# Moving operands as even and odd columns in two halves, read in turn by TensorE

## The chip, the cores and the metric

The kernel runs on one core of one Trainium2 chip. The metric is the device time of one execution in microseconds, as the median of several runs. Of one execution there is a hardware profile: a page, and a trace with every instruction's start and duration.

## The reference

A gated mix of an attention block and a gated feed-forward block over the same 2048 tokens of 512 numbers. 32 query heads of 16 share one key head and one value head; the feed-forward block is 1792 wide. Everything is float32.

```python
g = sigmoid((x * gate_w).sum(-1, keepdims=True))
q = (x @ wq).reshape(B, S, 32, 16).transpose(0, 2, 1, 3)
k, v = x @ wk, x @ wv
p = softmax(einsum("bhqd,bkd->bhqk", q, k) * 16 ** -0.5)
a = einsum("bhqk,bkd->bhqd", p, v).transpose(0, 2, 1, 3).reshape(B, S, 512) @ wo
b = (sigmoid(x @ w_gate) * (x @ w_up)) @ w_down
return g * a + (1 - g) * b
```

## The kernel before

**Numbers in two parts.** A float32 operand is split into a rounded part (type float32r, "hi") and the rest ("lo"), and a product is made as three products of these parts: hi x hi, hi x lo, lo x hi. The tiles that hold both parts have the shape [128, 2, 512]. float32r products are read by TensorE at one column after another without a second pass; plain float32 products show in the trace as two instructions each.

**Full-array products.** `project` (line 864) makes keys, values, the gate and the queries of a block of 512 tokens: 12 products of 128 rows by 512 moving columns, with `X[b, kc]` as the moving operand. `query_out` has ScalarE copy the queries out of PSUM; `store_q` sends them to memory, and `load_q` brings them back, stacked three times, into `stage`, which `stack` splits into `qs`.

**Paired products.** All else but the values uses one half of the array's rows (64 partitions), and two products, one on each half, go side by side as a pair:

- `maximum` (line 1126): 128 queries as the stationary operand against 512 keys (`ks`, moving); VectorE reduces each result of 128 x 512 to its row maxima (line 1128).
- `scores` (line 1135): 128 keys (stationary) against 512 queries (`qs`, moving), with the maxima subtracted by way of extra rows; ScalarE takes the exponential (line 1137) and writes `p`.
- `fill` (line 1105): gate and up products (`w` stationary, `x` or its copy with the halves exchanged, `xs`, moving), down products (`h` stationary, `wd` moving) and the attention's output products (`o` stationary, `wo` moving). ScalarE and VectorE take the results from PSUM (`gate`, `gated`, `part_of`).

**Values.** `pv` (line 1010) multiplies `p` (plain float32, 128 rows, moving) by `v_aug` in four column groups of the array, 32 columns each, side by side; eight instructions for one chunk of 128 keys and four heads. They come in runs of one to five chunks. Transposes (lines 934, 995) lie between them.

**Order.** A planner was run beforehand, and its outcome is a string `ORDER`, one character a step: `G` a full-array group, `V` a chunk of values, `C` the end of a sum, `T` the turning of maxima, and a hexadecimal digit for a pair, which tells what each half does (1 `maximum`, 2 `scores`, 3 `fill`). `plan()` goes through the string with costs for each engine and writes out the order of all instructions; at the end, each engine's instructions are chained in that order. The string, and thus the order, doesn't depend on what the chip does in a run: a step whose bank isn't free waits. PSUM has eight banks, each the target of one product group at a time, and a bank comes free when VectorE or ScalarE has read it.

**Layout.** `kernel` prepares the inputs on the host: x transposed in blocks of 512 tokens, the gate and up weights cut into column blocks, wo and wd as they are. Rows of 512 lie contiguously in SBUF, and the moving read goes through them from the first to the last.

Of the kernel before, what the change touches and what calls it, by code (L numbers as in the profile page):

```python
# [17 lines left out]
S, D, H, DH, F = 2048, 512, 32, 16, 1792  # L18
P = 128
TB = 512  # L20
NB = S // TB
NT = TB // P
KC = D // P
# [703 lines left out]
def tile_kernel(ctx, tc, x_in, wq, wkv, wo, wg, wu, wd, consts_in, out):  # L727
    nc = tc.nc
# [13 lines left out]
    banks = [pp.tile([P, 512], F32, tag=f"bank{i}", name=f"bank{i}") for i in range(8)]  # L742
# [18 lines left out]
    X, XS, XR = {}, {}, {}  # L761
# [48 lines left out]
    RAWS, WS = {}, {}  # L810
# [35 lines left out]
                hl = wp.tile([P, 2, 512], F32R, tag="wd", name=f"{name}_{k}", bufs=DB)  # L846
                WS[kind, b, 2 * i + k] = split(raw[r, k, :], hl[r], nc.gpsimd.tensor_copy, nc.gpsimd)

    full = slice(0, 512)
    part = lambda i: slice(i * P, (i + 1) * P)  # L850

    THREE = ((0, 0), (0, 1), (1, 0))
# [6 lines left out]
    def project(ps, w, b, order=BY_W, between=()):  # L859

        for i, (kc, (p, q)) in enumerate(order):
            if i < len(between):
                early(between[i])
            nc.tensor.matmul(ps, w[:, p, part(kc)], X[b, kc][:, q, :], start=i == 0, stop=i == 3 * KC - 1)  # L864


    wkv_c = fp.tile([P, TB], F32, tag="gs", name="wkv_raw", bufs=2)[:, :KC * 33]
# [15 lines left out]
    def early(n):  # L883

        for _ in range(n):
            nc.tensor.matmul(banks[7][:, :P], v_aug[:, :4, :], v_aug[:, 4:8, :], start=True, stop=True)
# [14 lines left out]
    ks = cp.tile([P, S], F32R, name="ks")  # L901
# [3 lines left out]
    qs_t = [cp.tile([P, 2, TB], F32R, name=f"qs{i}") for i in range(3)]  # L905
# [12 lines left out]
    def keys(b, _, ps):  # L918
        if b == 0:
            project(ps, wkv_s, b, BY_X, EARLY)  # L920
        else:
            project(ps, wkv_s, b)
# [26 lines left out]
    QD = {}  # L949

    def query(b, t, ps):
        project(ps, wq_s[t], b)

    def query_out(b, t, ps):
        QD[b, t] = ap.tile([P, TB], F32, tag="p", name=f"q{b}_{t}", bufs=PB)
        nc.scalar.copy(QD[b, t], ps)  # L956

    def store_q(b, t):

# [134 lines left out]
    def fill(h, j, at, i):  # L1094
        c, (p, q) = at // 3, THREE[at % 3]
        half = HALF[h]
        if j.kind in "gu":


            l, r = WS[j.key][half, p, part(c)], (X if c % 2 == h else XS)[j.b, c // 2][half, q, :]  # L1100
        else:
            c += 2 * FG[j.i // NT][0] if j.kind == "d" else KC - 1 if j.kind == "e" else 0
            l = (HS if j.kind == "d" else OT)[j.b, c][half, p, part(j.i % NT)]
            r = WS[j.kind, j.b, 0 if j.kind == "e" else c][half, q, :]
        nc.tensor.matmul(banks[i], l, r, start=at == 0, stop=at == j.n - 1)  # L1105

    def gate(h, j, i):
        GS[j.b, j.i, h] = fp.tile([P, TB], F32, tag="gs", name=f"gs{j.b}_{j.i}_{h}", bufs=2)
# [12 lines left out]
    def maximum(h, n, i):  # L1121
        s, pr = divmod(n, 2)
        u, n = divmod(s, NC)
        qt, kb = divmod(n, 4) if u else (n % 4, n // 4)
        r = slice(64 * h, 64 * h + 62)
        nc.tensor.matmul(banks[i], qs_t[u % 3][r, pr, part(qt)], ks[r, kb * 512:(kb + 1) * 512],  # L1126
                         start=True, stop=True)
        nc.vector.tensor_reduce(MX[u][:, pr, h, qt, kb:kb + 1], banks[i], axis=AX.X, op=ALU.max)  # L1128

    def scores(h, n, i):  # L1130
        e, pr = divmod(n, 2)
        pr = 1 - pr
        u, c = divmod(e, NC)
        r = HALF[h]
        nc.tensor.matmul(banks[i], ks[r, part(c)], qs_t[u % 3][r, pr, :], start=True, stop=True)  # L1135
        p = PT[u, c, 2 * pr + h] = ap.tile([P, 512], F32, tag="p", name=f"p{u}_{c}_{pr}_{h}", bufs=PB)
        nc.scalar.activation(p, banks[i], AF.Exp, scale=0.25)  # L1137

    on_bank = lambda act: lambda *args: act(*args[:-1], banks[args[-1]])
    acts = {  # L1140
        "load_x": first_x, "x_first": first_hi, "xf": first_lo, "wq_first": wq_hi, "wq": wq_lo, "keys": on_bank(keys),
        "query": on_bank(query), "turn": on_bank(turn), "keys_out": on_bank(keys_out), "query_out": on_bank(query_out),
        "turned": on_bank(turned), "store_q": store_q, "load_q": load_q, "stack": stack,
        "load": load_item, "w_hi": w_hi, "w": w_split, "x_hi": x_hi, "x": x_lo, "turn_x": turn_x,
        "f": fill, "gate": gate, "gated": gated, "h": h_split, "part": part_of, "add": add_part, "out": send_out,
        "m": maximum, "max_finish": max_finish, "max_turn": max_turn, "send_max": send_max, "s": scores,
        "values": on_bank(pv), "sums_out": on_bank(sums_out), "sum_add": sum_add, "store": store, "sums": sums, "invert": invert, "send_inverse": send_inverse,
        "spread": spread, "divide": divide,
# [10 lines left out]
    ps = rest[3:]  # L1159
# [5 lines left out]
    o = []  # L1165
# [9 lines left out]
        nc.scalar.copy(o[i], rest[2 - i][:, 2 * P:3 * P])  # L1175
    for t in range(NT):
        r = HALF[t % 2]
        nc.tensor.matmul(ps[t], o[t // 2][r], WS["last"][r], start=True, stop=True)  # L1178
    for t in (0, 1, 2, 3):

        ba, scale = BA[NB - 1, t], gsig[:, n0 + t:n0 + t + 1]
# [10 lines left out]
    last = {}  # L1192
# [46 lines left out]
```

## Time and profile before

| | |
|---|---|
| median of 3 runs | 1591.24 us (1591.23 to 1591.73) |
| span of the profiled execution, first to last instruction | 1588.7 us |
| TensorE busy, weight loads busy | 1580.4 us, 1003.2 us |
| VectorE, ScalarE, GpSimd busy | 1410.7, 1186.8, 905.5 us |
| mean granted clock of TensorE | 1.000 |
| moved by DMA | 98.13 MB |

The profile's page gives the span, which leaves out what lies before the first and behind the last instruction; the runs' times hold it. A busy TensorE means that a product was under way, not that the array took a column at every clock: products are pipelined, and the start of one to the start of the next says more than a duration. In the rows, PE is TensorE's products, PEld its weight loads, DVE VectorE, ACT ScalarE, POOL GpSimd. A group's row gives the line, the engine, the operation, the tiles as out<-in, the shapes, the count, then busy time in us and the mean duration in ns, and the engine's idle time ahead of these instructions with what ended it. A timeline row gives start and duration in us. A row of stretches gives, for each engine, the busy time and the count of instructions, then the granted clock, the share of the DMA engines' time and GB/s.

### The profile page before, as it was taken

How to read it: one execution, taken by the hardware profiler on the slowest of the kernel's cores; microseconds unless marked ns; L12 is line 12 of the kernel's file. 1: busy time of each engine (PE TensorE's matmuls, PEld its weight loads, DVE VectorE, ACT ScalarE, POOL GpSimd, SP SyncE). 2: the span in 40 equal slices, each digit the busy share in tenths (PEclk: the TensorE clock that was granted, in tenths of full speed). 3: DMA queues.
4: the chain of work that ended last, by engine and by line, in shares of the span. 5: the costliest groups of instructions: out<-in, count | busy, mean ns of one | idle time of the engine just before them, and what ended most of it. 6: DMA issues, size and time to landing. Idle time of an engine off the chain costs nothing.

```text
span 1588.7 us, 33698 instructions
## 1 busy us (share of the span) xinstructions
PE 1580.4 (99%) x12950; PEld 1003.2 (63%) x12950; DVE 1410.7 (89%) x2450; ACT 1186.8 (75%) x2349; POOL 905.5 (57%) x703
## 2 busy tenths in 40 slices
PE   9999999999999999999999999999999999999998
PEld 7767666556655666665755666666565566666644
DVE  6999899999899999998988989998998998989962
ACT  5277767688688767788769776788877876777897
POOL 5347565756753664675582666465766366468242
PEclk9999999999999999999999999999999999999999
DMA  7312111123110221114121211111512021110011
GB/s 239 138 49 75 55 37 41 59 68 101 52 58 23 86 63 40 55 42 109 51 72 32 84 43 55 35 58 32 134 32 81 24 83 59 29 59 31 9 35 45
DMA packets 52231, 98.13 MB, mean 62 GB/s; under 512 B 17960, under 2 KB 19240, under 8 KB 51044
## 3 DMA queue, kind: packets, MB, share of 16 engines
q1 hardware_dynamic: 52068, 95.96, 19.7%
q8 instruction: 102, 1.67, 0.4%
q14 instruction: 61, 0.50, 0.1%
HBM read 74.05 MB, written 8.90 MB: 52 GB/s over the span
## 4 chain that ended last, share of the span: by engine, by line
PE 99%; DMA 0%; ACT 0%; SPq 0%; DVE 0%; issue 0%; DVEq 0%; ACTq 0%
PE bank L1105 33%; PE bank L1010 30%; PE bank L1126 16%; PE bank L1135 16%; PE bank L864 3%; DMA wqr<-wq 0%; PE bank L995 0%; PE bank L1178 0%; SPq L767 0%; PE bank L934 0%; ACT x L782 0%; DVE ba L1187 0%; DVEq L1235 0%; ACT wq L910 0%; ACT q L956 0%
## 5 line engine op out<-in xcount | busy, mean ns | idle before, releaser
L1128 DVE TENSOR_REDUCE mx<-bank 128x1 f32<-128x512 f32 x2048 | 1261.2, 683 | 114.5 <-PE bank L1126 62.2
L1137 ACT ACTIVATE p<-bank 128x512 f32<-128x512 f32 x2048 | 1032.5, 656 | 35.6 <-PE bank L1135 18.6
L1135 PE MATMUL bank<-qs,ks 64*128 64x512 f32 x2048 | 713.7, 405 | 0.0
L1126 PE MATMUL bank<-ks,qs 62*128 62x512 f32 x2048 | 691.1, 405 | 0.0
L1010 PE MATMUL bank<-p,v_aug 128*32 128x512 f32 x4096 | 485.1, 598 | 0.0
L1135 PEld LDWEIGHTS bank<-qs,ks 64*128 64x128 f32 x2048 | 350.5, 185 | 133.2 <-DVE mx L1128 44.1
L1126 PEld LDWEIGHTS bank<-ks,qs 62*128 62x128 f32 x2048 | 348.6, 185 | 112.0 <-DVE mx L1128 31.3
L1018 ACT COPY ou<-bank 128x512 f32<-128x512 f32 x131 | 77.1, 589 | 299.1 <-PE bank L1010 236.2
L1105 PE MATMUL bank<-wd,hl 64*128 64x512 f32 x1344 | 272.2, 391 | 0.0
L1010 PEld LDWEIGHTS bank<-p,v_aug 128*32 128x32 f32 x4096 | 110.6, 109 | 248.5 <-issue 214.1
L1105 PEld LDWEIGHTS bank<-wd,hl 64*128 64x128 f32 x1344 | 199.0, 185 | 15.3 <-DVE mx L1128 0.2
L1021 POOL TENSOR_TENSOR ou<-ou,ou 128x512 f32<-128x512 f32 x104 | 134.3, 1292 | 98.3 <-ACT ou L1018 94.5
L1105 PE MATMUL bank<-xs,wg 64*128 64x512 f32 x672 | 184.6, 391 | 0.0
L1105 PE MATMUL bank<-xs,wu 64*128 64x512 f32 x672 | 183.7, 392 | 0.0
L1105 PE MATMUL bank<-x,wg 64*128 64x512 f32 x672 | 182.4, 391 | 0.0
L1105 PE MATMUL bank<-x,wu 64*128 64x512 f32 x672 | 181.3, 393 | 0.0
L982 POOL TENSOR_TENSOR qs<-stage,qs 16x1024 fp32r<-16x1024 f32 x62 | 148.4, 2393 | 4.8
L1105 PEld LDWEIGHTS bank<-x,wu 64*128 64x128 f32 x672 | 111.0, 185 | 10.2 <-DVE mx L1128 1.7
L1105 PEld LDWEIGHTS bank<-x,wg 64*128 64x128 f32 x672 | 112.5, 185 | 6.7
L1105 PEld LDWEIGHTS bank<-xs,wu 64*128 64x128 f32 x672 | 112.6, 185 | 6.4
L1105 PEld LDWEIGHTS bank<-xs,wg 64*128 64x128 f32 x672 | 112.3, 185 | 5.6
L757 POOL CAST hl<-h 128x512 fp32r<-128x512 f32 x56 | 34.2, 611 | 142.4 <-DVE h L1115 142.2
(92 smaller groups left out, 1159.6 us busy)
## 6 DMA issues: line engine op xcount, KB each, us to landing
rg<-wg SPq DMA_DIRECT2D x28, 512.0 KB
ru<-wu SPq DMA_DIRECT2D x28, 512.0 KB
rd<-wd SPq DMA_DIRECT2D x28, 512.0 KB
stage<-qd SPq DMA_DIRECT2D x192, 64.0 KB
xs<-x SPq DMA_DIRECT2D x16, 512.0 KB
xf<-x_in SPq DMA_DIRECT2D x16, 256.0 KB
qd<-q SPq DMA_DIRECT2D x16, 256.0 KB
ra<-wo SPq DMA_DIRECT2D x8, 512.0 KB
```

The source lines that it names most:

```text
L757: hi(hl[:, 0, :], raw)
L864: nc.tensor.matmul(ps, w[:, p, part(kc)], X[b, kc][:, q, :], start=i == 0, stop=i == 3 * KC - 1)
L982: e.tensor_tensor(qs[r], stage[r], f32(qs[r]), op=ALU.subtract)
L1010: nc.tensor.matmul(ps[32 * j:32 * j + 32, :], v_aug[:, c, :], PT.pop((u, c, j)), start=new, stop=last)
L1018: (nc.scalar.copy if e == "act" else nc.vector.tensor_copy)(OU[i], ps)
L1021: nc.gpsimd.tensor_tensor(OU[n], OU[n], OU[i], op=ALU.add)
L1105: nc.tensor.matmul(banks[i], l, r, start=at == 0, stop=at == j.n - 1)
L1126: nc.tensor.matmul(banks[i], qs_t[u % 3][r, pr, part(qt)], ks[r, kb * 512:(kb + 1) * 512], start=True, stop=True)
L1128: nc.vector.tensor_reduce(MX[u][:, pr, h, qt, kb:kb + 1], banks[i], axis=AX.X, op=ALU.max)
L1135: nc.tensor.matmul(banks[i], ks[r, part(c)], qs_t[u % 3][r, pr, :], start=True, stop=True)
L1137: nc.scalar.activation(p, banks[i], AF.Exp, scale=0.25)
```

## The change

The moving operands of `project`, `fill`, `maximum`, `scores` and the last output products are read through `turned_round`, a view of a row of 512 as 256 x 2 with the step of 256 innermost: TensorE reads element 0, 256, 1, 257, and so on. For x, wo and wd the host lays out the rows so that even columns fill the first half and odd ones the second, and the products come out in natural order as before. The queries are put into that layout by the ScalarE copy in `query_out`, whose destination is now written in turn in two halves (PSUM is read in order). The keys `ks` lie as before; `maximum` reads them in another order, which leaves a row's maximum as it is. Stationary operands are read contiguously as before; in `maximum` a slice of 128 columns of `qs` now holds every second query, and the maxima go back into `qs` in the same layout. The moving operands of the values, and of the transposes, are untouched. `ORDER` and the planner's costs are untouched.

```diff
-    full = slice(0, 512)
+    turned_round = lambda a: a.rearrange("p (a b) -> p b a", a=2)
...
-            nc.tensor.matmul(ps, w[:, p, part(kc)], X[b, kc][:, q, :], start=i == 0, stop=i == 3 * KC - 1)
+            nc.tensor.matmul(ps, w[:, p, part(kc)], turned_round(X[b, kc][:, q, :]), start=i == 0,
+                             stop=i == 3 * KC - 1)
...
-        nc.scalar.copy(QD[b, t], ps)
+        nc.scalar.copy(turned_round(QD[b, t]), ps.rearrange("p (b a) -> p b a", a=2))
...
-        nc.tensor.matmul(banks[i], l, r, start=at == 0, stop=at == j.n - 1)
+        nc.tensor.matmul(banks[i], l, turned_round(r), start=at == 0, stop=at == j.n - 1)
...
-        nc.tensor.matmul(banks[i], qs_t[u % 3][r, pr, part(qt)], ks[r, kb * 512:(kb + 1) * 512],
+        nc.tensor.matmul(banks[i], qs_t[u % 3][r, pr, part(qt)], turned_round(ks[r, kb * 512:(kb + 1) * 512]),
                          start=True, stop=True)
...
-        nc.tensor.matmul(banks[i], ks[r, part(c)], qs_t[u % 3][r, pr, :], start=True, stop=True)
+        nc.tensor.matmul(banks[i], ks[r, part(c)], turned_round(qs_t[u % 3][r, pr, :]), start=True, stop=True)
...
-        nc.tensor.matmul(ps[t], o[t // 2][r], WS["last"][r], start=True, stop=True)
+        nc.tensor.matmul(ps[t], o[t // 2][r], turned_round(WS["last"][r]), start=True, stop=True)
...
+    two = lambda w: c(np.asarray(w).reshape(-1, TB // 2, 2).transpose(0, 2, 1).reshape(-1, TB))
-        "x_in": c(np.asarray(A_x)[0].reshape(NB, TB, D).transpose(0, 2, 1).reshape(NB * D, TB)),
+        "x_in": two(np.asarray(A_x)[0].reshape(NB, TB, D).transpose(0, 2, 1).reshape(NB * D, TB)),
...
-        "wo": c(np.asarray(A_wo)),
+        "wo": two(A_wo),
...
-        "wd": c(np.asarray(B_w_down)),
+        "wd": two(B_w_down),
```

## The prediction

> **What bounds the kernel now.** I read the page first (busy shares, the slices, the chain that ended last), then the chain in order of time for single pieces, then the timeline of TensorE and VectorE where work is dense, then the stretches.
>
> ```profile
> span 1588.7 us, 33698 instructions
> PE 1580.4 (99%) x12950; PEld 1003.2 (63%) x12950; DVE 1410.7 (89%) x2450; ACT 1186.8 (75%) x2349; POOL 905.5 (57%) x703
> ...
> PEclk9999999999999999999999999999999999999999
> ...
> PE 99%; DMA 0%; ACT 0%; SPq 0%; DVE 0%; issue 0%; DVEq 0%; ACTq 0%
> PE bank L1105 33%; PE bank L1010 30%; PE bank L1126 16%; PE bank L1135 16%; PE bank L864 3%; DMA wqr<-wq 0%; PE bank L995 0%; PE bank L1178 0%; SPq L767 0%; PE bank L934 0%; ACT x L782 0%; DVE ba L1187 0%; DVEq L1235 0%; ACT wq L910 0%; ACT q L956 0%
> ```
>
> The reader is to see that the chain is TensorE from end to end, at full granted clock. Lines 1105, 1126 and 1135 are the paired products (65% of the span), 864 the full-array ones (3%); line 1010, the values (30%), is not touched by the change. VectorE, at 89%, stands close behind. The span is 2.5 us below the median of the runs, 1591.24 us; I add these 2.5 us to whatever I work out for the span.
>
> How many products are touched: the counts of the groups.
>
> ```profile
> L1135 PE MATMUL bank<-qs,ks 64*128 64x512 f32 x2048 | 713.7, 405 | 0.0
> L1126 PE MATMUL bank<-ks,qs 62*128 62x512 f32 x2048 | 691.1, 405 | 0.0
> L1010 PE MATMUL bank<-p,v_aug 128*32 128x512 f32 x4096 | 485.1, 598 | 0.0
> L1105 PE MATMUL bank<-wd,hl 64*128 64x512 f32 x1344 | 272.2, 391 | 0.0
> ...
> L1105 PE MATMUL bank<-xs,wg 64*128 64x512 f32 x672 | 184.6, 391 | 0.0
> L1105 PE MATMUL bank<-xs,wu 64*128 64x512 f32 x672 | 183.7, 392 | 0.0
> L1105 PE MATMUL bank<-x,wg 64*128 64x512 f32 x672 | 182.4, 391 | 0.0
> L1105 PE MATMUL bank<-x,wu 64*128 64x512 f32 x672 | 181.3, 393 | 0.0
> L1105 PE MATMUL bank<-wa,o 64*128 64x512 f32 x360 | 71.0, 392 | 0.0
> L864 PE MATMUL bank<-x,wq 128*128 128x512 f32 x192 | 47.4, 398 | 0.2 <-ACT wq L910 0.2
> L864 PE MATMUL bank<-x,wkv_s 128*128 128x512 f32 x48 | 12.7, 406 | 0.1
> ```
>
> Line 1105 adds up to 4392 (with 12 more in a group not shown), so (4404 + 2048 + 2048) / 2 = 4250 pairs, and 192 + 48 = 240 full-array products. A pair is two products, one on each half of the array, that run side by side.
>
> What one costs is read from starts, not from the 391 ns, which hold a pipeline's depth. First the ends of a stretch of pairs without a break, then the stretch's count; behind them nine full-array products in a row, four transposes of 128 columns, and two runs of the values.
>
> ```profile
> 316.44 0.39 PE L1135 MATMUL bank<-qs,ks 64*128 64x512 f32 x1
> ...
> 328.09 0.43 PE L1126 MATMUL bank<-ks,qs 62*128 62x512 f32 x2
> ```
> ```profile
> 316.45:328.12 11.67, 11.67 (x103) 1.00 0.14 45
> ```
> ```profile
> 39.67 2.21 PE L864 MATMUL bank<-x,wkv_s 128*128 128x512 f32 x9
> ...
> 60.97 0.60 PE L934 MATMUL bank<-consts,vt 128*128 128x128 f32 x4
> ```
> ```profile
> L934 PE MATMUL bank<-consts,vt x16: 270/273/328, 19.7 to 61.3; 128*128 128x128 f32 x16
> ```
> ```profile
> 163.21 3.57 PE bank L1010 x32
> 176.41 4.43 PE bank L1010 x40
> ```
>
> The stretch counts 103, two of them begun before 316.44; from the first to the 101st are 50 pairs in 328.09 - 316.44 = 11.65 us: **233 ns a pair**. A full-array product: (2.21 - 0.39) / 8 = **227 ns**, taking off one duration of 0.39 (the pairs' mean above). Both read 512 columns. The values tell what reading costs at another pace: 8 instructions more take 4.43 - 3.57 = 0.86 us, which is two rounds of four side by side, 430 ns for the same 512 columns. The transposes, also plain float32, take (0.60 - 0.27) / 3 = 110 ns for 128 columns (0.27 us lasts one of them, by the middle figures of its row). So plain float32 costs (430 - 110) / 384 = 0.833 ns a column and about 3 ns an instruction. At twice that pace 512 columns would be 213 + 3 = 216.5 ns. The products at full pace take 227 and 233: **10.5 and 16.5 ns over**, which the half-paced ones don't show.
>
> **The change part by part.** Nothing is added or removed as an instruction, and no queue is passed: transfers keep their sizes and counts, since x_in, wo and wd are laid out by the host, and stationary operands are read as before. Three things differ.
>
> *The moving read.* Each touched product reads column 0 from the first half of its row, column 1 from the second, 1024 bytes on, and so on; each half is thus read at half pace. No instruction of the trace reads so, and I bound it by the nearest rows. From below: the 216.5 ns just worked out, if a half-paced read loses nothing, as in the values. That takes 4250 x 16.5 + 240 x 10.5 = 70 + 2.5 = 72.6 us from TensorE's work. From above: 430 ns, the values' round, if each jump costs a slot of the read: 4250 x (430 - 233) + 240 x (430 - 227) = 837 + 49 = 886 us more. I take 216.5: the excess is found only where one contiguous stream is read at full pace, and two streams at half pace are, each by itself, what the values' operand is. Both ends are kept.
>
> [...]
>
> *The copy of q.* It now writes its 512 results in turn into two halves.
>
> ```profile
> L956 ACT COPY q<-bank 128x512 f32<-128x512 f32 x16 | 9.4, 586 | 31.2 <-PE bank L864 31.2
> ```
>
> 16 of them, 9.4 us in all. Cheaper it can't well be; dearer at most, by my estimate, twice (another slot for each element): 9.4 us on ScalarE. It waited 31.2 us for TensorE in these places, which hides a copy of twice the length. Behind it stand only the store of q and the bank. I take zero, and 9 us for the range.
>
> *What is late next.* A faster TensorE asks for free banks sooner, and the order is fixed. VectorE frees half of them:
>
> ```profile
> L1128 DVE TENSOR_REDUCE mx<-bank 128x1 f32<-128x512 f32 x2048 | 1261.2, 683 | 114.5 <-PE bank L1126 62.2
> ```
> ```profile
> 1168.98 8.50 DVE L1128 TENSOR_REDUCE mx<-bank 128x1 f32<-128x512 f32 x14 [1.27 <-PE bank L1126]
> ```
> ```profile
> 323.39 7.88 DVE L1128 TENSOR_REDUCE mx<-bank 128x1 f32<-128x512 f32 x13
> 333.41 0.69 DVE L1128 TENSOR_REDUCE mx<-bank 128x1 f32<-128x512 f32 x1 [2.15 <-PE bank L1135]
> ```
> ```profile
> 0.00:50.00 50.00, 48.40 (x224) 36.36 (x224) 34.21 (x60) 23.55 (x40) 26.24 (x23) 1.00 0.78 242
> ...
> 1500.00:1550.00 50.00, 50.00 (x400) 23.94 (x400) 35.52 (x61) 47.24 (x96) 22.08 (x21) 1.00 0.09 28
> 1550.00:1588.70 38.70, 32.10 (x243) 15.75 (x239) 10.62 (x18) 28.23 (x58) 11.26 (x10) 0.99 0.16 46
> ```
>
> VectorE is idle for 1588.7 - 1410.7 = 178 us; 15.8 + 14.5 + 28.1 = 58 of them lie at the two ends, so 120 us lie between 50 and 1500 us. They aren't spread evenly: fourteen reductions run without a gap in 8.50 us (607 ns each), thirteen in 7.88, and the idle time comes while TensorE runs values, when VectorE has emptied every bank it was given (2.15 us in the second fence). So between two runs of values VectorE is nearly saturated, and TensorE's lead turns into waits for banks. What can be kept is that values start with one more full bank behind them, and VectorE's idle time shrinks. In 40 pairs the lead is 40 x 16.5 = 0.66 us, about one reduction (0.61); there are eight banks, one of them the values' own. Kept at all: between none and 72.6 us (that fits into the 120). I take a third, 24 us: a lead of one reduction is kept where a bank was still free, and the gapless rows say that this is the smaller part. Where ScalarE is the tighter one (47.24 of 50 us from 1500 on) it is the same.
>
> Sum: 1588.7 - 24 + 0 (q) + 0 (transfers) = 1564.7, and 2.5 around it: **1567 us**.
>
> **The rivals.**
>
> *The turned read costs a slot for each column (slower).* Place: every touched product. Price: 886 us as above, 1591 + 886 = 2477 us, or a little less, since waits for banks go. [...] It decides early: each ns on a pair is 4.25 us, so a pair of 234 ns is already slower by over 0.2% (3.2 us). A small version, 1 to 11 ns on a pair, gives 1595 to 1640 us.
>
> *The excess is not the read's, or all of it is swallowed (no change).* Then pairs stay at 233 ns, or TensorE only waits more. For it: the pair takes 6 ns more than the full-array product, so some of the excess comes from two products sharing the array, and VectorE's gapless rows; against: the 120 us of idle VectorE. 1591 us.
>
> *All of the lead is kept.* 1591 - 73 = 1518 us; against it stand those same rows of VectorE. It is the far end of the forecast's own range.
>
> **How the numbers follow.** Faster as forecast: 0.58, own range 1538 to 1587 (54 to 4 us kept). No change: 0.17. Small slowing, to 1640: 0.07. Half pace, 2477: 0.18. What can't be told from no change is taken as 0.2%, 3.2 us. So faster 0.58, same 0.17, slower 0.25. The range leaves out the half-paced case and 0.02 at the low end: 1535 to 1640. The likeliest is 1567.
>
> **What would show it.** Right: starts of pairs in an unbroken stretch some 217 ns apart and of full-array products too, values unchanged at 430 ns a round, VectorE busy with the same 1411 us in a shorter span, and new idle time of the weight loads that the reductions of line 1128 and the exponentials of line 1137 end. Wrong in the read: pairs at 400 ns or more and VectorE below 65% (1411 of some 2477 is 57%), or at 233 with nothing else moved. Wrong in the share kept: pairs at 217 but a span above 1585 (less kept than I say) or below 1540 (the plan had more room than the gapless rows suggest). Wrong in q: copies of line 956 above 586 ns with waits of the full-array products behind them.

## The result, and the profile after

The changed kernel takes 1571.6 us (median of 4 runs, 1571.44 to 1572.96) against 1591.5 us before (now the median of 4 runs): 0.9877 of the time, with a 95% interval of 0.9863 to 0.9891. That is 19.9 us or 1.2% faster. Its profiled execution has a span of 1569.5 us, 19.2 us under that of before. Line numbers from 865 on are one higher than before.

The page of the changed kernel, the lines that answer to those shown of before:

```profile
span 1569.5 us, 33698 instructions
PE 1559.6 (99%) x12950; PEld 980.0 (62%) x12950; DVE 1402.1 (89%) x2450; ACT 1191.4 (76%) x2349; POOL 899.9 (57%) x703
...
PEclk9999999999999999999999999999999999999999
...
PE 96%; DVE 3%; ACT 0%; DMA 0%; SPq 0%; issue 0%; DVEq 0%; ACTq 0%
PE bank L1011 30%; PE bank L1106 29%; PE bank L1136 17%; PE bank L1127 16%; PE bank L864 3%; DVE mx L1129 3%; DMA xf<-x_in 0%; PE bank L996 0%; PE bank L1179 0%; ACT q L957 0%; ACT p L1138 0%; DVE ba L1066 0%; DMA qs<-mt 0%; ACT x L782 0%; SPq L767 0%
```

TensorE's busy time has gone down with the span, the work of VectorE, ScalarE and GpSimd is within 1% of what it was, and in the chain 3% has passed to VectorE's reductions (line 1129): there are now places where TensorE waits for them. The chain gives ScalarE's exponentials (line 1138) 0%; the experiments show that TensorE waits for them too. The pace shows in the timeline of TensorE, here at the end of the stretch whose rows of before the prediction quotes, and in a full-array group:

```profile
322.59 0.38 PE L1127 MATMUL bank<-ks,qs 62*128 62x512 f32 x1
322.59 0.38 PE L1106 MATMUL bank<-x,wg 64*128 64x512 f32 x1
322.81 0.38 PE L1127 MATMUL bank<-ks,qs 62*128 62x512 f32 x1
322.81 0.38 PE L1106 MATMUL bank<-x,wg 64*128 64x512 f32 x1
323.02 0.38 PE L1127 MATMUL bank<-ks,qs 62*128 62x512 f32 x1
323.02 0.38 PE L1106 MATMUL bank<-x,wg 64*128 64x512 f32 x1
```
```profile
41.82 2.86 PE L864 MATMUL bank<-x,wq 128*128 128x512 f32 x12
```

Pairs start (323.02 - 322.59) / 2 = 215 ns apart, in step to 10 ns; the full-array group takes 2.86 - 0.38 = 2.48 us from its first start to its last, which is ten steps of 216 ns and one of 320. But the whole stretch of 50 pairs, from 311.71 to 323.24 us, takes 11.53 us, where before it took 11.65: unhindered it would be 50 x 0.216 = 10.8. What may hold it is seen in ScalarE's timeline of the same stretch, before and after, and in a row of the stretch after (busy time and count for PE, PEld, DVE, ACT, POOL):

```profile
316.30 0.59 ACT L1018 COPY ou<-bank 128x512 f32<-128x512 f32 x1 [4.22 <-PE bank L1010]
316.79 2.08 ACT L1137 ACTIVATE p<-bank 128x512 f32<-128x512 f32 x4
318.70 0.73 ACT L1086 ACTIVATE pa_d<-bank,gom 128x512 f32<-128x512 f32 x1
319.27 8.49 ACT L1137 ACTIVATE p<-bank 128x512 f32<-128x512 f32 x17
327.50 1.42 ACT L1109 ACTIVATE gs<-bank 128x512 f32<-128x512 f32 x2
```
```profile
311.58 0.58 ACT L1019 COPY ou<-bank 128x512 f32<-128x512 f32 x1 [4.12 <-PE bank L1011]
312.06 2.07 ACT L1138 ACTIVATE p<-bank 128x512 f32<-128x512 f32 x4
313.98 0.73 ACT L1087 ACTIVATE pa_d<-bank,gom 128x512 f32<-128x512 f32 x1
314.55 8.49 ACT L1138 ACTIVATE p<-bank 128x512 f32<-128x512 f32 x17
322.71 1.35 ACT L1110 ACTIVATE gs<-bank 128x512 f32<-128x512 f32 x2
```
```profile
312.00:323.30 11.30, 11.30 (x102) 9.43 (x98) 11.30 (x19) 11.30 (x24) 5.67 (x5) 1.00 0.15 47
```

There is no idle time in brackets from the first exponential on: 17 exponentials take 8.49 us without a gap, in both kernels. VectorE has no gap in these 11.30 us either, so this stretch alone doesn't tell which of the two holds TensorE. ScalarE's 75% on the page is the mean of stretches of pairs, where it's full, and of runs of values, where it waits (4.22 us in the first row). The weight loads' waits say the same; the columns are the total, the count and the longest, in us, before and then after:

```profile
PEld bank L1135 <- DVE mx L1128: 44.1, 55, 0.8
PEld bank L1126 <- DVE mx L1128: 31.3, 40, 0.8
PEld bank L1135 <- ACT p L1137: 21.7, 36, 0.8
PEld bank L1126 <- ACT p L1137: 16.6, 34, 0.8
```
```profile
PEld bank L1136 <- ACT p L1138: 51.1, 182, 0.8
PEld bank L1136 <- DVE mx L1129: 45.7, 68, 0.8
PEld bank L1127 <- ACT p L1138: 35.7, 126, 0.8
PEld bank L1127 <- DVE mx L1129: 30.7, 41, 0.8
```

Waits that end with an exponential: 36 + 34 = 70 before, 182 + 126 = 308 after. Waits that end with a reduction: 95 and 109. (The loads' idle time in these four rows of after, 163 us, is more than the 45 us of the lead that the experiments give for waits; these are counts, not lost time.)

What TensorE itself loses shows when the steps between starts of pairs are averaged by their place behind a run of values, over the whole trace. The first step takes 335 ns before and 320 after; steps two to six 232 and 217; those from the twenty-first on 233 and 233. So the lead is whole for the first pairs of a stretch, and on average nothing is left of it from the twenty-first on. Apart from first steps, 16 steps of 290 ns or more are found before, and 246 after.

### The profile page after: what moved, and what is told of

It reads as the page before. It is cut to its first block, busy times and chain, and to the rows that moved or that the text cites. A ratio compares the mean times of both kernels' runs of the same rounds, so it can differ in the third digit from the quotient of the medians.

```text
span 1569.5 us, 33698 instructions
## 1 busy us (share of the span) xinstructions
PE 1559.6 (99%) x12950; PEld 980.0 (62%) x12950; DVE 1402.1 (89%) x2450; ACT 1191.4 (76%) x2349; POOL 899.9 (57%) x703
## 4 chain that ended last, share of the span: by engine, by line
PE 96%; DVE 3%; ACT 0%; DMA 0%; SPq 0%; issue 0%; DVEq 0%; ACTq 0%
PE bank L1011 30%; PE bank L1106 29%; PE bank L1136 17%; PE bank L1127 16%; PE bank L864 3%; DVE mx L1129 3%; DMA xf<-x_in 0%; PE bank L996 0%; PE bank L1179 0%; ACT q L957 0%; ACT p L1138 0%; DVE ba L1066 0%; DMA qs<-mt 0%; ACT x L782 0%; SPq L767 0%
## 5 line engine op out<-in xcount | busy, mean ns | idle before, releaser
L1127 PE MATMUL bank<-ks,qs 62*128 62x512 f32 x2048 | 682.7, 400 | 0.0
L1136 PEld LDWEIGHTS bank<-qs,ks 64*128 64x128 f32 x2048 | 345.2, 184 | 162.1 <-ACT p L1138 51.1
L1106 PE MATMUL bank<-wd,hl 64*128 64x512 f32 x1344 | 266.3, 382 | 0.0
L1106 PEld LDWEIGHTS bank<-wd,hl 64*128 64x128 f32 x1344 | 193.3, 186 | 8.2 <-DVE mx L1129 0.5
L1106 PE MATMUL bank<-xs,wu 64*128 64x512 f32 x672 | 179.1, 381 | 0.0
L1106 PE MATMUL bank<-x,wg 64*128 64x512 f32 x672 | 177.8, 381 | 0.0
L1106 PE MATMUL bank<-x,wu 64*128 64x512 f32 x672 | 176.3, 382 | 0.0
```

Source lines behind the costliest of these rows:

```text
L1106: nc.tensor.matmul(banks[i], l, turned_round(r), start=at == 0, stop=at == j.n - 1)
L1127: nc.tensor.matmul(banks[i], qs_t[u % 3][r, pr, part(qt)], turned_round(ks[r, kb * 512:(kb + 1) * 512]), start=True, stop=True)
L1136: nc.tensor.matmul(banks[i], ks[r, part(c)], turned_round(qs_t[u % 3][r, pr, :]), start=True, stop=True)
```

## The experiments

**The reads by themselves.** A kernel of its own, no change of this one: chains of 40 products without evictions, one for each way in which the 512 moving columns are read.

```python
VIEWS = {
    "seq": lambda a: a,
    "halves": lambda a: a.rearrange("p (a b) -> p b a", a=2),              # 0, 256, 1, 257
    "quarters": lambda a: a.rearrange("p (a b) -> p b a", a=4),            # 0, 128, 256, 384, 1
    "near": lambda a: a.rearrange("p (c a b) -> p c b a", a=2, b=4),       # 0, 4, 1, 5, 2, 6
    "sixtyfour": lambda a: a.rearrange("p (c a b) -> p c b a", a=2, b=16), # 0, 16, 1, 17
    "two": lambda a: a.rearrange("p (b a) -> p a b", a=2),                 # 0, 2, 4, 6
    "four": lambda a: a.rearrange("p (b a) -> p a b", a=4),                # 0, 4, 8, 12
    "sixteen": lambda a: a.rearrange("p (b a) -> p a b", a=16),            # 0, 16, 32, 48
}
```

> The computation is replaced: chains of 40 products alone, without evictions, one chain for each way of reading the 512 moving columns: in sequence; two halves in turn (1 KB apart); four quarters in turn; neighbouring 16-byte lines in turn; neighbouring 64-byte blocks in turn; every second, fourth, sixteenth column. Each for pairs on half the rows, for the full array (float32r), and for plain float32 in four column groups. My theory (contiguous reading at full pace loses 10 to 17 ns in 512 columns, two streams at half pace lose nothing): in sequence 227 to 233 ns a product, halves and quarters 216; plain float32 430 ns a round in sequence and in halves. Rival A (the excess belongs to the surroundings in the kernel, such as evictions and transfers): 216 for all reads alone. Rival B (it is only that successive columns lie far apart in memory): neighbouring lines in turn stay at 227 to 233 while halves are 216. [...]

Its timeline; each row is one chain, with its start and its length in us (40 products on the full array, 40 pairs, or 10 plain float32 products in four column groups):

```profile
26.75 8.80 PE L55 MATMUL bank<-pair_halves,w 64*128 64x512 f32 x80
...
117.89 9.37 PE L59 MATMUL bank<-full_seq,w 128*128 128x512 f32 x40
127.10 8.79 PE L59 MATMUL bank<-full_halves,w 128*128 128x512 f32 x40
135.73 11.49 PE L59 MATMUL bank<-full_quarters,w 128*128 128x512 f32 x40
147.05 8.80 PE L59 MATMUL bank<-full_near,w 128*128 128x512 f32 x40
155.69 8.80 PE L59 MATMUL bank<-full_sixtyfour,w 128*128 128x512 f32 x40
164.32 18.21 PE L59 MATMUL bank<-full_two,w 128*128 128x512 f32 x40
182.35 18.63 PE L59 MATMUL bank<-full_four,w 128*128 128x512 f32 x40
200.80 17.51 PE L59 MATMUL bank<-full_sixteen,w 128*128 128x512 f32 x40
218.25 8.79 PE L64 MATMUL bank<-cols_seq,wr 128*32 128x512 f32 x80
226.85 11.04 PE L64 MATMUL bank<-cols_halves,wr 128*32 128x512 f32 x80
...
276.97 9.50 PE L64 MATMUL bank<-cols_two,wr 128*32 128x512 f32 x80
```

Less the last product's 0.38 to 0.64 us and divided by 39, the full-array chains give: in sequence 230 ns, halves 216, neighbouring pieces of 16 bytes 216, of 64 bytes 216, quarters 283, every second column 451, every fourth 461, every sixteenth 433. Pairs in halves take (8.80 - 0.38) / 39 = 216 too. (In sequence most steps are 227 ns; a single one of 337 makes the mean 230.) So the excess belongs to the read in sequence and is there without evictions or transfers (rival A falls), and distance plays no part, since columns 16 bytes apart do as well as halves, 1 KB apart (rival B falls). My theory holds for float32r in halves, and fails beside them: four streams are slower than one (283 ns), and plain float32 in column groups, which was to be unmoved at 430 ns a round, goes from 430 to 540 ns in halves, from the start of a round to the start of the next. A half-paced stream is not free as such; two streams in turn happen to be, for float32r (216 ns). Why every second, fourth or sixteenth column takes 433 to 461 ns, no run shows.

**Cheaper evictions, four ways.** The maxima take 256 columns of 512, the exponentials 256 (and the values read these twice), in both kernels together, and in the changed one also one at a time. With halved exponentials the softmax is no longer the reference's. Each of these kernels was run once; the 4 to 7 runs of a kernel with full evictions lie within 2 us of each other:

```diff
-        nc.vector.tensor_reduce(MX[u][:, pr, h, qt, kb:kb + 1], banks[i], axis=AX.X, op=ALU.max)
+        nc.vector.tensor_reduce(MX[u][:, pr, h, qt, kb:kb + 1], banks[i][:, :256], axis=AX.X, op=ALU.max)
...
-        nc.scalar.activation(p, banks[i], AF.Exp, scale=0.25)
+        nc.scalar.activation(p[:, :256], banks[i][:, :256], AF.Exp, scale=0.25)
...
-            nc.tensor.matmul(ps[32 * j:32 * j + 32, :], v_aug[:, c, :], PT.pop((u, c, j)),
+            nc.tensor.matmul(ps[32 * j:32 * j + 32, :], v_aug[:, c, :], PT.pop((u, c, j))[:, :256].unsqueeze(1).to_broadcast([P, 2, 256]),
```

> The kernel before, with evictions halved: the maxima take only 256 of 512 columns and the exponentials too (the values read those 256 twice), so the softmax is not the reference's. Theory (what was lost went to waits for banks): this removes the waits of before, which are some 26 us in pair steps, so 1560 to 1570 us. Rival (weight loads, not banks, take the lost part): about the same here, it tells nothing alone; it is the base for the next run.

> The changed kernel with the same halved evictions. Theory (the lead is 72 us and was lost to waits for banks that VectorE and ScalarE free too late): the distance to the kernel before with halved evictions is 60 to 75 us, so 1490 to 1505 us. Rival (a product of 216 ns leaves its successor's weight load of 185 ns too little room, so the lead is lost in TensorE's own sequence): the distance stays at 20 to 35 us, so 1530 to 1545 us.

> The changed kernel with only the exponentials halved (the values read 256 columns twice), VectorE's reductions whole. Theory one (VectorE, the busier one, frees the banks too late, as the prediction said): little, 1560 to 1571 us. Theory two (the new waits end with the exponentials: 308 of them in the trace of after against 70 before, while those that end with reductions are 109 against 95): most of the lost part returns, 1520 to 1545 us.

> The changed kernel with only the reductions of the maxima halved (256 of 512 columns), exponentials whole. With both halved it took 1520.6 us, with the exponentials alone 1556.3. Theory one (VectorE holds the banks, since it is nearly gapless between values): most of the lost part returns, 1525 to 1545 us. Theory two (banks circulate through both engines in turn, and either alone gives little): 1550 to 1568 us, and both together more than the sum of the two.

| | full evictions | halved reductions | halved exponentials | both halved |
|---|---|---|---|---|
| before | 1591.5 us | | | 1585.3 us |
| changed | 1571.6 us | 1571.7 us | 1556.3 us | 1520.6 us |

With cheap evictions the change is worth 1585.3 - 1520.6 = 64.8 us, with the real ones 19.9: 45 us, two thirds of the lead, go to waits for banks, and the rival (weight loads of 185 ns in TensorE's own sequence) falls. The values keep their 430 ns a round in all four (in the three of the changed kernel 32 instructions take 3.57 us, 40 take 4.43). The distance is within the theory's 60 to 75 us, but both times are above their forecasts, since the kernel before gained only 6 us, not 20 to 30: nearly all its late steps are the first ones behind values, and these stay at 335 ns with halved evictions, so they are no waits for banks. In the changed kernel the late steps elsewhere fall from 246 to 6, and pairs take 217 ns at every place behind the first. Each engine alone tells the order in which they bind. VectorE's halved reductions bring nothing at all, ScalarE's halved exponentials 15.3 us, both 51 us, more than the two gains added up, as theory two of the last run has it. ScalarE binds first; once it is freed, VectorE does. Both single runs missed my numbers: 1556.3 lies between the two theories' ranges for ScalarE's run, and 1571.7 is above both of those for VectorE's. The waits of the weight loads in the two runs, halved reductions first, then halved exponentials:

```profile
PEld bank L1136 <- ACT p L1138: 60.8, 222, 0.8
PEld bank L1136 <- DVE mx L1129: 20.1, 24, 0.8
```
```profile
PEld bank L1136 <- DVE mx L1129: 68.6, 162, 0.8
PEld bank L1136 <- ACT p L1138: 15.1, 18, 0.8
```

With short reductions 222 of these waits end with an exponential (182 in the changed kernel) and 24 with a reduction (68). With short exponentials it is the other way round: 18 end with an exponential, 162 with a reduction.

**The copy of q, turned where it reads.** ScalarE reads PSUM with a step of two columns and writes in order; the result is the same.

```diff
-        nc.scalar.copy(turned_round(QD[b, t]), ps.rearrange("p (b a) -> p b a", a=2))
+        nc.scalar.copy(QD[b, t].rearrange("p (a b) -> p a b", a=2), ps.rearrange("p (b a) -> p a b", a=2))
```

> The changed kernel with the copy of q turned at its source: ScalarE reads PSUM with a step of two columns and writes SBUF in order, the same result. In the trace of after the copy takes 1070 ns (586 before). Theory (the turned write costs the time, a strided read of PSUM does not): 586 to 650 ns a copy, and 0 to 4 us less in all, 1568 to 1572 us. Rival (PSUM read with a step costs as much): 1000 ns or more, no change.

The group's row in the changed kernel and in this one:

```profile
L957 ACT COPY q<-bank 128x512 f32<-128x512 f32 x16 | 17.1, 1070 | 24.2 <-PE bank L864 24.1
```
```profile
L957 ACT COPY q<-bank 128x512 f32<-128x512 f32 x16 | 9.4, 586 | 28.8 <-PE bank L864 28.8
```

The turned write costs 484 ns a copy, the turned read of PSUM nothing. The time: 1571.3 us (1570.69 to 1572.23), ratio to before 0.9874 (0.9857 to 0.989), which can't be told from the changed kernel's. The 7.7 us of ScalarE's work lie in the 24 to 29 us that it waits for the full-array products there.

**The fills alone.** `turned_round` in line 1105 only, in the kernel before; the rows keep their natural order, so these products' columns come out in another one.

```diff
-        nc.tensor.matmul(banks[i], l, r, start=at == 0, stop=at == j.n - 1)
+        nc.tensor.matmul(banks[i], l, turned_round(r), start=at == 0, stop=at == j.n - 1)
```

> The kernel before with only fill's moving operands read in turned halves (rows stay in natural order, so the columns of these products come out in another order). Theory (each half of the array goes at its own pace, but products start in order, so a pair goes at the slower one's): only pairs of two fills gain, some 900 of 4250 pairs by 16 ns, a lead of 15 us, of which a quarter to a half is kept: 1583 to 1588 us. Rival (each turned product takes its own share): half of the change's lead and gain, 1579 to 1583 us.

1583.1 us, from a single run, just inside the first range and next to the second; the time can't decide, the timeline does. A piece of it, TensorE alone:

```profile
302.48 0.39 PE L1135 MATMUL bank<-qs,ks 64*128 64x512 f32 x1
302.48 0.38 PE L1105 MATMUL bank<-x,wu 64*128 64x512 f32 x1
302.70 0.38 PE L1105 MATMUL bank<-xs,wu 64*128 64x512 f32 x1
302.72 0.39 PE L1126 MATMUL bank<-ks,qs 62*128 62x512 f32 x1
302.91 0.38 PE L1105 MATMUL bank<-xs,wu 64*128 64x512 f32 x1
302.95 0.39 PE L1135 MATMUL bank<-qs,ks 64*128 64x512 f32 x1
```

The fills follow at 302.48, 302.70, 302.91 (215 ns), the products of the other half at 302.48, 302.72, 302.95 (235 ns): each half of the array goes at its own pace, and the quicker one runs ahead (what stops it was not followed). Over the whole trace, steps of pairs behind the first and under 290 ns average 225 ns, 232 before. These 7 ns on every pair are about half of the 16; the theory's 900 pairs at 16 ns would make 3.4. The rival holds: 8.4 us of the 19.9 (against the 1591.5 us of before) for 4404 of the 8740 touched products.

**An order for the faster TensorE.** The experiments point to the order: ScalarE and VectorE are full between values (no gap in the 11.30 us above) and idle in long runs of them (4.22 us of ScalarE in the rows above, 2.15 us of VectorE in the prediction's). The planner's costs other than those of pairs and full-array groups were scaled by 1.08 (233 / 216), and the string was improved piece by piece by its sum. The products are those of the changed kernel, but not all are paired as before: `f`, two fills, stands 991 times for 901. The string also has 40 more ends of sums (`C`), and 1513 marks `.`, at which the planner lets time pass without a step, for 5.

```diff
+for _n in ("LATE LATE_A FREE FREE_A RED GATED SUM ENDS PARTS INVERSE EXP COPY SCALED TAIL TAIL_A SEEN IN OUT "
...
+    globals()[_n] = slower(globals()[_n])
...
-    "GGGGGGGG555G555G555G555GG555G55G555GG555G55GG555G555G555GTff7ff5f5dG6e6fdfedeedfe7bdbf9b7fbd9ffb7f775VVVC9b7b77b"
...
```

> The changed kernel with ORDER improved piece by piece for the faster TensorE: the planner's costs other than TensorE's steps are scaled by 1.08 (233 / 216 ns), and stretches between runs of values are put in another order where the planner's sum gets shorter, with the same contents. Runs of values get shorter: 180 of 290 are single chunks, 85 of 220 before. Theory (ScalarE and VectorE are full between values and idle in long runs of them, so shorter runs keep more of the lead): some 10 us less than the changed kernel, 1558 to 1565 us. Rival (what binds is the evictions' work itself, whatever the order): 1569 to 1573 us.

> The same new order with the layout of before (233 ns a pair). Theory: the order spends TensorE's lead on 70 more switches between values and pairs, so without the lead it is no better than the old order, 1590 to 1605 us. Rival (the order is simply better, for any pace): 1575 to 1588 us.

With the turned layout 1568.9 us (1568.75 to 1570.06), ratio to before 0.9859 (0.9843 to 0.9876): the quickest with full evictions, by 2.7 us, though its interval overlaps the changed kernel's. With the layout of before 1611.5 us in a single run, 20 more than the old order gives and above both of my ranges: without the lead the new order only costs. The page of the new order with the turned layout, and its weight loads' waits:

```profile
PE 1557.4 (99%) x12950; PEld 970.2 (62%) x12950; DVE 1408.3 (90%) x2453; ACT 1216.0 (78%) x2386; POOL 949.2 (61%) x743
```
```profile
PEld bank L1170 <- DVE mx L1163: 48.4, 63, 0.8
PEld bank L1161 <- DVE mx L1163: 46.1, 63, 0.8
PEld bank L1170 <- ACT p L1172: 41.4, 120, 0.8
PEld bank L1161 <- ACT p L1172: 31.7, 74, 0.8
```

Waits that end with an exponential fall from 308 to 194. Added up over the starts of TensorE's instructions, the time from one paired product to the next falls from 945 to 922 us, but the values with the changes to and from pairs rise from 538 to 560. In the trace there are 275 runs of values for 222, so 53 more (17 of the 290 counted in the expectation are only parted by the end of a sum): 0.4 us each. With the layout of before the values rise by as much, from 537 to 561 us, and the pairs gain only 3. The time lies between my two ranges, 0.1 us below the rival's: pairs do gain from another order, but nearly all of it goes into the switches.

## Why the prediction was right

*The read.* The prediction took 216.5 ns for a product read in halves, from half of the plain float32 round; 216 was measured, alone and in the kernel. The number was right, the reason only in part: plain float32 in halves got dearer (540 for 430 ns), so half pace is no warrant, and it was partly luck that the number came out. The rival of a slot for each column (2477 us) did not come; what it priced does exist, at 433 to 461 ns, but for reads with a step, not for two streams in turn. Neighbouring pieces of 16 bytes, read in turn, take 216 ns as the halves do.

*The lead.* Forecast 72.6 us; 64.8 measured with cheap evictions. There the step of a pair behind the first falls from 231.5 to 217.0 ns, 14.5 where the prediction took 16.5 from one stretch that was a little slower than the rest.

*The share kept.* Forecast a third, 24 us; measured 19.9, which is 31% of 64.8. The third was chosen between none and all and not worked out, so that it came this close is luck. Its mechanism, a lead that is kept where a bank is still free, fits the trace: 217 ns in steps two to six behind values, 233 from the twenty-first on. Calling 1518 us, with all of the lead kept, the far end of its own range was a slip, since that range ends at 1538. The step that failed is who takes the rest. The prediction named VectorE, from its gapless reductions, and gave ScalarE one sentence. ScalarE binds first, as halved reductions (no gain) and halved exponentials (15.3 us) show; VectorE comes behind it. The trace of before had it: the ScalarE rows above, 17 exponentials in 8.49 us without a gap. The prediction quotes its 75% on the page, a mean over two kinds of stretches; it took VectorE's mean apart in this way, and ScalarE's only from 1500 us on. "VectorE nearly saturated between values" was right as far as it went.

*The copy of q.* Taken at nothing, and at most twice as long: it is 1.83 times as long, and costs nothing in the time.

*The 6 ns of a pair beyond a full-array product*, which the prediction gave to two products that share the array, are gone as well: both take 216 ns. Sharing alone doesn't cost them, since a chain of pairs in sequence, by itself, settles at 227 ns like one of full-array products. Why pairs in the kernel took 232 in sequence stays open.

## What to carry to other kernels

An engine's busy share over a span says little where stages alternate: take a stretch of the stage in question and look for brackets of idle time, in every engine that frees what the bound engine needs. When work is planned tightly, making the bound engine faster paid here only the part that the next two engines could follow (19.9 of 64.8 us); halving their work, one at a time and together, tells which binds and how much is behind it. The order of a moving read is worth a chain of products by itself before a layout is built around it.

## What was not expected of the hardware

For float32r, 512 columns in sequence take 227 ns by themselves, two places read in turn 216, whether 16 bytes or 1 KB apart, four in turn 283, and a step of 2, 4 or 16 columns 433 to 461. Plain float32 in four column groups prefers the sequence: 430 ns a round, 540 in halves, some 460 at a step of two. Why two in turn are quicker than one stream was not found. ScalarE reads PSUM at a step of two columns at no cost (586 ns, as in sequence), but takes 1070 ns where it writes SBUF in two halves in turn.
